# Weights on the sync queue in column blocks, a layer norm in three lagged steps, and one product for the memory read, in a fused attention and gated-MLP block

## The chip, the cores and the metric

The kernel runs on one core of one Trainium2 chip. The metric is device time in microseconds of one execution; the time before is the median of three runs. The engines in the profile are PE (matmul), PEld (its weight loads), DVE (vector), ACT (scalar activations), POOL (GpSimd) and SP (which here only issues transfers; SPq and ACTq are the queues of SP and ACT).

## The reference, cut to what matters

The input x has 2048 tokens of 1024 channels, in bfloat16. With 32 heads of width 32 and four segments of 512 tokens:

```python
h = x + A(layernorm(x));  out = h + B(layernorm(h))

# A, for each segment s: causal softmax attention inside the segment, and a linear memory over earlier ones
p = softmax(q_s k_s^T * scale + mask);  a_dot = p v_s
a_mem = (phi(q_s) M) / (phi(q_s) z + 1e-6)          # phi(t) = t+1 if t>0 else exp(t)
o = g * a_mem + (1 - g) * a_dot                      # g = sigmoid(beta), one per head
M += phi(k_s)^T v_s;  z += sum(phi(k_s))             # afterwards: A returns o @ wo

# B, with F = 3584, Fh = 1792
z = gelu(x @ w_in);  z1 = z[:, :Fh];  z2 = layernorm(z[:, Fh:])
return (z1 * (w_sp @ z2 + b_sp)) @ w_out
```

## The kernel before

Every operation is recorded by a small helper (so that all of them carry line 209 in the profile), which derives the waits from the memory cells that an operation reads and writes; a PSUM bank of 2 KB is one cell, so engines that touch different columns of a bank still wait for each other. Each engine runs its own operations in the order of recording. The order of the code is thus the order on each engine, and nothing is rearranged.

**Start.** `x_load` brings chunks of 128 tokens into `XCH` on SP; the weights are issued on ACT's queue, whole or in halves. For the four chunks of segment 0, `ln_stats` takes mean and variance on DVE and the reciprocal root on POOL, `ln_apply` normalizes on DVE, `pe_T` transposes on PE with an eviction by ACT into `XNT`, and `proj_v` makes half of V. `gates` prepares the gate masks.

**Attention loop.** The loop over n = 0..31 takes eight rounds for each of four segments (s, c = divmod(n, 8)); a round treats four heads. In a round, in this order: `logits(n, 0)`, the key product for round n+1, `pv(n-1, 2)` with the output norm of the round before (`norm`, on DVE), a pop of the background list, `logits(n, 1)`, the query product for n+1, `pv(n, 0)`, `logits(n, 2)` with the memory read (`mem` on PE, `mem_norm` on DVE, from segment 1 on), the list f3, `phi(n+1)`, `pv(n, 1)`, a pop, `state(n)` (the memory update), the list f4, a pop. Logits of four key blocks stand in banks 0 to 3, the values' products in banks 4 and 5; the projections and the state rotate over banks 6 and 7. Each `logits` is followed by an exponential on ACT (tiles e_99, e_100, e_101 for parts 0, 1, 2) and causal masks on POOL (`affine_select`). `mem` uses columns 256 on of banks 0 to 2, whose first 256 columns hold part 2 of the logits: for each of four query blocks one product with 128 columns for the numerator and one with four for the denominator.

f3 and f4 hold the V halves of this or the next segment (`proj_v`), and the output projection of the segment before (`wo`, halves of 512 columns), which adds x (`XR`), stores h, and hands the chunk to a layer norm whose transpose lands in `HNT`. In the first four rounds of segments 0 to 2, a chunk of the next segment is loaded and handed to the same background list:

```python
def ln_tasks(src, dst, tcl):
    box = {}
    bg.append(lambda: box.__setitem__("k", ln_stats(src)))
    bg.append(lambda: to_T(dst, tcl, ln_apply(src, box["k"])))
```

`bg_pop` runs one entry. `to_T` is a transposing transfer issued by SP. SP also issues the key transposes at the end of `phi`, the x loads, the stores of h, and the w_in blocks (`win_load`).

**Feed-forward part.** After the loop, `z2_group(k, tc)` multiplies a chunk of normalized h by 448 columns of w_in (eight matmuls), applies gelu on ACT, and takes statistics on DVE, for 4 x 16 groups; the last wo pieces of segment 3 stand between groups 5 to 8 of the first pass. Then come the z1 products, the product with w_sp, and w_out. Tiles of this part lie over those of the attention part in SBUF.

Of the kernel before, what the change touches and what calls it, by code (L numbers as in the profile page):

```python
# [18 lines left out]
NTC = T // 128  # L19
NQ = 8  # L20
SCALE = 32 ** (-0.5)
LN_EPS = 1e-5
MEM_EPS = 1e-6
# [234 lines left out]
def bass_sequential_preLN__memory_aug_infini_attn__mixer_gmlp__prompt_kernel(  # L258
# [43 lines left out]
    cb = Bump(0, 14 * K)  # L302
# [11 lines left out]
    STATS = [cb("stats%d" % i, [128, 2, 6], F32) for i in range(2)]  # L314
    MV = [cb("mv%d" % i, [128, 2], F32) for i in range(2)]
    RS = [cb("rs%d" % i, [128, 2], F32) for i in range(2)]
    RD = cb("rd", [128, 4, 4], F32)
    RDM = cb("rdm", [128, 4, 4], F32)

# [3 lines left out]
    XNT = [tens("xnT0", [128, 8, L], BF16, 30 * K), tens("xnT1", [128, 8, L], BF16, 38 * K)]  # L323
# [7 lines left out]
    LNO = [b1("lno%d" % i, [128, D], BF16) for i in range(3)]  # L331
    OT = b1("oT", [128, NQ, L], BF16)
    b2 = Bump(134 * K, ARENA)
    XCH = [b2("xch%d" % i, [128, D], BF16) for i in range(3)]
    QK = [b2("qk%d" % i, [128, 2, L], BF16) for i in range(3)]
    PQK = [b2("pqk%d" % i, [128, 2, L], BF16) for i in range(3)]
    ETMP = b2("etmp", [128, 2, L], BF16)
# [3 lines left out]
    TM = b2("tm", [128, 4, 4, 32], F32)  # L341
# [29 lines left out]
    def next_bank():  # L371
        b = rot["banks"][rot["n"] % len(rot["banks"])]
        rot["n"] += 1
        return b

    def mm8(dst, lhs, rhs, n=8):
        for i in range(n):
            pe.matmul(dst, lhs(i), rhs(i), start=(i == 0), stop=(i == n - 1))


    def x_load(tc):
        sp.dma_start(XCH[tc % 3][:], x2d[tc * 128:(tc + 1) * 128, :])
# [12 lines left out]
    act.dma_start(WO[:], wcols(A_wo, 0, D))  # L395


    pool.memset(MHALF[:], -0.5)
# [22 lines left out]
    lnc = [0]  # L421

    def ln_stats(src):
        k = lnc[0] % 2
# [93 lines left out]
    def mem(n):  # L518
        c = n % NQ
        for cq in range(4):  # L520
            pq = PQK[n % 3][:, 0, cq * 128:(cq + 1) * 128]
            o = 256 + (cq % 2) * 128
            pe.matmul(PS[:, cq // 2, o:o + 128], pq, MZB[:, c, :, 0:32], start=True, stop=True)
            pe.matmul(PS[:, 2, 256 + cq * 4:260 + cq * 4], pq, MZB[:, c, :, 32], start=True, stop=True)

    def mem_norm(n):
        dve.tensor_single_scalar(RDM[:], PS[:, 2, 256:272].rearrange("p (q i) -> p q i", i=4), float(MEM_EPS),
                                 ALU.add)
        dve.reciprocal(RDM[:], RDM[:])
        om = PS[:, 0:2, 256:512].rearrange("p b (h i d) -> p b h i d", h=2, i=4)  # L530
# [50 lines left out]
    bg = []  # L581

    def ln_tasks(src, dst, tcl):
        box = {}
        bg.append(lambda: box.__setitem__("k", ln_stats(src)))
        bg.append(lambda: to_T(dst, tcl, ln_apply(src, box["k"])))

    def bg_pop(k=1):
        for _ in range(k):
            if bg:  # L590
                bg.pop(0)()


    ks = {}
    ks[0] = ln_stats(XCH[0])
# [16 lines left out]
    def win_load(k):  # L612
        kind, lo, w = CH[k]
        sp.dma_start(WIN[k % 3][:, :, 0:w], wcols(B_w_in, lo, lo + w))


    LAST = NSEG * NQ - 1
    for n in range(LAST + 1):
        s, c = divmod(n, NQ)
        f3, f4 = [], []  # L620
        if s == 0:
            f3 = [("v", 0, c, 1)] if c < 4 else [("v", 1, c - 4, 0)]
        elif s < NSEG - 1:
            if c < 2:
                f3, f4 = [("v", s, 2 * c, 1)], [("v", s, 2 * c + 1, 1)]
            elif c < 6:
                f3, f4 = [("wo", s - 1, c - 2, 0)], [("wo", s - 1, c - 2, 1)]
            else:
                f3, f4 = [("v", s + 1, 2 * (c - 6), 0)], [("v", s + 1, 2 * (c - 6) + 1, 0)]
        else:  # L630
            if c < 4:
                f3 = [("v", s, c, 1)]
            wl = {2: [0], 3: [1], 4: [2], 5: [3], 6: [4, 5], 7: [6, 7]}.get(c, [])
            for u in wl:
                f4.append(("wo", s - 1, u // 2, u % 2))

        def fill(lst):
            for u in lst:
                (proj_v if u[0] == "v" else wo)(*u[1:])

        if s < NSEG - 1 and c < 4:
            x_load(4 * (s + 1) + c)
            ln_tasks(XCH[(4 * (s + 1) + c) % 3], XNT[(s + 1) % 2], c)
        if s > 0 and c == 1:
            xr_load(4 * (s - 1))

        logits(n, 0)
        if n < LAST:
            proj_qk(n + 1, 1)
        if n > 0:  # L650
            pv(n - 1, 2)
        bg_pop()
        logits(n, 1)
        if n < LAST:
            proj_qk(n + 1, 0)
# [13 lines left out]
    xr_load(4 * (NSEG - 1))  # L669


    rot["banks"] = list(range(8))
    win_load(2)

    def wsp_load(tb):
# [4 lines left out]
    zq = []  # L680

    def z2_group(k, tc):
        s, tcl = divmod(tc, 4)
        b = next_bank()
        wi = WIN[k % 3]
        mm8(PS[:, b, 0:448], lambda i: HNT[s][:, i, tcl * 128:(tcl + 1) * 128], lambda i: wi[:, i, 0:448])
        z = Z2[:, tc, k * 448:(k + 1) * 448]
        act.activation(z, PS[:, b, 0:448], ACTF.Gelu_apprx_tanh)
        dve.bn_stats(ZST[:, tc, k, :], z)
        if k == 3:  # L690
            dve.bn_aggr(ZMV[:, tc, :], ZST[:, tc, :, :])
            pool.tensor_single_scalar(ZRS[:, tc:tc + 1], ZMV[:, tc, 1:2], float(LN_EPS), ALU.add)
            pool.tensor_tensor(ZRS[:, tc:tc + 1], ZRS[:, tc:tc + 1], MHALF[:], ALU.pow)
            zq.append(tc)

    def z2_apply():
        tc = zq.pop(0)
        dve.tensor_scalar(Z2[:, tc, :], Z2[:, tc, :], ZMV[:, tc, 0:1], ZRS[:, tc:tc + 1], ALU.subtract, ALU.mult)

    for k in range(4):  # L700
        for tc in range(NTC):
            z2_group(k, tc)
            if k == 0:
                bg_pop()
                if 5 <= tc < 9:
                    wo(NSEG - 1, tc - 5, 0)
                    wo(NSEG - 1, tc - 5, 1)
                    bg_pop()
            if len(zq) > 1:
                z2_apply()  # L710
        if k + 3 < 8:
            win_load(k + 3)
        assert not bg
    for k in range(4, 8):
        lo, w = CH[k][1:]
        for fl in range(w // 128):
# [64 lines left out]
```

## Time and profile before

| | |
|---|---|
| median of 3 runs | 865.43 us (862.6 to 865.89) |
| profiled execution | 867.66 us, its span 865.9 us |
| PE busy | 802.0 us, 93% of the span |
| DVE, ACT, POOL busy | 382.9, 302.2, 121.8 us |
| start until the first logits | 38.22 us |
| attention loop, to the first w_in product | 38.22 to 363.54 us |
| feed-forward part | 363.54 to 865.90 us |

A row of the timeline has the start, the duration, the engine, the line, the operation, the tile written and those read (buffer numbers belong to the tile's number: e_99, e_100 and e_101 are three buffers), the count where neighbours are merged, and in brackets the idle time before it with what ended it. A wait is read from the brackets; whether it costs anything is read from PE, whose idle time alone makes the end later. PE's time for a merged group runs to the end of the last matmul's pipeline, so two groups behind one another take less than the sum.

### The profile page before, as it was taken

What the parts mean: (1) busy time and instruction counts of PE and PEld (TensorE: products, weight loads), DVE (VectorE), ACT (ScalarE), POOL (GpSimd) and SP (SyncE); (2) the same over time, 40 slices, a digit from 0 to 9 for tenths busy, and PEclk for the clock granted to TensorE, in tenths of its full rate; (3) what the DMA queues carried; (4) which work ended last, traced back from release to release, by engine and by line L of the source; (5) the groups of instructions that cost most, each with busy time, mean ns of one, the idle gap of its engine ahead of it and who ended that gap; (6) DMA issues with size and microseconds to landing.
All of it is one profiled execution on the core that took longest, in us unless ns stands there. A gap on an engine that the chain in (4) does not pass through costs nothing.

```text
span 865.9 us, 12541 instructions
## 1 busy us (share of the span) xinstructions
PE 802.0 (93%) x5354; PEld 390.6 (45%) x5440; DVE 382.9 (44%) x777; ACT 302.2 (35%) x351; POOL 121.8 (14%) x234
## 2 busy tenths in 40 slices
PE   1787988899889999699999999999999999999998
PEld 0343544444444555345555444444444444444443
DVE  4153347876787456665446400005314323432432
ACT  1566866677667778313333333310000000000000
POOL 2033322332233324100003200000000000000000
PEclk9998999999999999899999999999999999999999
DMA  8422042435343304373100420056035026002002
GB/s 317 138 62 50 20 93 67 111 73 86 81 109 71 75 6 134 81 168 101 49 21 29 122 48 1 1 178 108 7 90 105 0 62 139 1 31 73 1 7 79
DMA packets 122728, 64.79 MB, mean 75 GB/s; under 512 B 94768, under 2 KB 109616, under 8 KB 122672
## 3 DMA queue, kind: packets, MB, share of 16 engines
q1 hardware_dynamic: 117472, 55.60, 26.9%
q10 hardware_dynamic: 5200, 8.39, 2.7%
q8 instruction: 42, 0.69, 0.3%
q14 instruction: 14, 0.11, 0.0%
HBM read 32.51 MB, written 8.39 MB: 47 GB/s over the span
## 4 chain that ended last, share of the span: by engine, by line
PE 78%; DVE 7%; ACT 5%; POOL 3%; DMA 3%; ACTq 2%; issue 2%; SPq 1%
PE ps L209 78%; ACTq L209 2%; POOL e_100 L209 2%; DMA xch_87<-in_A_x_dram 1%; ACT e_99 L209 1%; DVE stats_59 L209 1%; ACT v L209 1%; ACT e_100 L209 1%; SPq L209 1%; DVE stats_60 L209 1%; DMA xch_88<-in_A_x_dram 1%; ACT etmp L209 1%; POOL rs_63 L209 1%; DVE etmp L209 1%; ACT e_101 L209 0%
## 5 line engine op out<-in xcount | busy, mean ns | idle before, releaser
L209 PE MATMUL ps<-w_out,yT 128*128 128x512 bf16 x439 | 96.9, 379 | 0.5
L209 PE MATMUL ps<-wspT_113,z_110 128*128 128x512 bf16 x439 | 96.5, 379 | 0.5
L209 PE MATMUL ps<-wspT_112,z_110 128*128 128x512 bf16 x439 | 96.5, 379 | 0.5
L209 ACT ACTIVATE e_99<-ps 128x2048 bf16<-128x2048 f32 x32 | 60.0, 1875 | 45.9 <-PE ps L209 45.9
L209 PEld LDWEIGHTS ps<-wspT_113,z_110 128*128 128x128 bf16 x448 | 43.9, 98 | 52.8
L209 PEld LDWEIGHTS ps<-wspT_112,z_110 128*128 128x128 bf16 x448 | 43.8, 98 | 52.9
L209 PEld LDWEIGHTS ps<-w_out,yT 128*128 128x128 bf16 x448 | 43.8, 98 | 52.9
L209 ACT ACTIVATE z_110<-ps 128x448 bf16<-128x448 f32 x64 | 34.8, 543 | 85.2 <-PE ps L209 85.2
L209 DVE TENSOR_TENSOR tmpg_119<-ps,brow_117 128x512 f32<-128x512 f32 x14 | 9.7, 690 | 116.7 <-DMA brow_117<-in_B_b_sp_dram 96.4
L209 PE MATMUL ps<-wo,oT 128*128 128x512 bf16 x241 | 57.7, 385 | 3.8 <-DVE hch_80 L209 1.2
L209 ACT ACTIVATE e_100<-ps 128x2048 bf16<-128x2048 f32 x32 | 60.1, 1877 | 0.8 <-PE ps L209 0.7
L209 DVE BATCH_NORM_STATS2 zst<-z_110 128x6 f32<-128x448 bf16 x64 | 39.8, 622 | 41.5 <-ACT z_110 L209 41.5
L209 ACT ACTIVATE z1T<-ps 128x512 bf16<-128x512 f32 x56 | 33.4, 597 | 63.3 <-PE ps L209 63.3
L209 PE MATMUL ps<-wv,xnT_71 128*128 128x512 bf16 x121 | 30.5, 396 | 16.1 <-ACT xnT_71 L209 15.2
L209 POOL TENSOR_SCALAR_AFFINE_SELECT e_100<-e_100 128x512 bf16<-128x512 bf16 x64 | 41.1, 666 | 26.6 <-ACT e_100 L209 26.6
L209 PE MATMUL ps<-v,e_100 128*128 128x33 bf16 x512 | 22.4, 178 | 17.4 <-POOL e_100 L209 16.9
L209 PEld LDWEIGHTS ps<-wo,oT 128*128 128x128 bf16 x256 | 23.7, 99 | 29.4 <-issue 1.9
L209 ACT ACTIVATE e_101<-ps 128x1024 bf16<-128x1024 f32 x32 | 32.7, 1023 | 11.0 <-PE ps L209 10.7
L209 PE MATMUL ps<-xnT_71,wk 128*128 128x512 bf16 x125 | 32.7, 409 | 1.6 <-DVE msum L209 0.9
L209 POOL TENSOR_SCALAR_AFFINE_SELECT e_99<-e_99 128x512 bf16<-128x512 bf16 x32 | 20.5, 639 | 95.7 <-ACT e_99 L209 95.7
L209 ACT ACTIVATE v<-ps 128x512 bf16<-128x512 f32 x32 | 19.1, 597 | 40.3 <-PE ps L209 40.3
L209 PE MATMUL ps<-xnT_72,wk 128*128 128x512 bf16 x126 | 30.0, 380 | 1.3 <-DVE msum L209 0.9
(187 smaller groups left out, 1103.3 us busy)
## 6 DMA issues: line engine op xcount, KB each, us to landing
w_out<-in_B_w_out_dram SPq DMA_DIRECT2D x1, 3584.0 KB, 13.0
wv<-in_A_wv_dram ACTq DMA_DIRECT2D x2, 1024.0 KB, 14.0
wk<-in_A_wk_dram ACTq DMA_DIRECT2D x1, 2048.0 KB, 14.5
wq<-in_A_wq_dram ACTq DMA_DIRECT2D x1, 2048.0 KB, 19.3
wo<-in_A_wo_dram ACTq DMA_DIRECT2D x1, 2048.0 KB, 17.3
xr_77<-in_A_x_dram SPq DMA_DIRECT2D x8, 256.0 KB, 3.0
xr_78<-in_A_x_dram SPq DMA_DIRECT2D x8, 256.0 KB, 3.1
win_107<-in_B_w_in_dram SPq DMA_DIRECT2D x2, 896.0 KB, 4.7
```

Of the source, the lines that this page charges most:

```text
L209: ins = getattr(e, op.name)(*op.args, **op.kw)
```

## The change

- Start: x chunks 0 and 1, then the first half of wv, chunks 2 and 3, the first 256 columns of wk and of wq, beta, and the rest of the weights, all issued by SP in this order. `XCH` has four buffers instead of three, so the tiles laid out behind it move by 2 KB. Statistics of chunks 0 and 1 stand ahead of the first apply.
- Layer norm in the loop: three lists, one for each step (statistics; reciprocal root on POOL; apply and transpose). Each pop runs one entry of each list, the oldest step first, so a chunk's three steps lie one pop apart. Statistics tiles have four buffers instead of two.
- Memory read: one product of 132 columns for each query block (numerator and denominator side by side), in banks 0 to 3; in `mem_norm` one multiply over four blocks instead of two over two.
- Last segment: the wo pieces of rounds 28, 29 stand in f3 instead of f4, those of round 30 in f3 and f4 instead of both in f4; in round 31 the wo pieces stand where the next round's key and query products would, and the first two w_in groups in f3 and f4.
- After the loop the banks rotate from 6, 7, 0, 1 on; the first pass begins with group 2; w_in statistics run behind by two groups; there is one more pop between the wo halves.

```diff
-    XCH = [b2("xch%d" % i, [128, D], BF16) for i in range(3)]
+    XCH = [b2("xch%d" % i, [128, D], BF16) for i in range(4)]
...
     x_load(0)
+    x_load(1)
+    sp.dma_start(WV[:, :, 0:512], wcols(A_wv, 0, 512))
+    x_load(2)
+    x_load(3)
+    sp.dma_start(WK[:, :, 0:256], wcols(A_wk, 0, 256))
+    sp.dma_start(WQ[:, :, 0:256], wcols(A_wq, 0, 256))
     sp.dma_start(BETAB[:], A_beta.partition_broadcast(128))
-    x_load(1)
-    x_load(2)
-    act.dma_start(WV[:, :, 0:512], wcols(A_wv, 0, 512))
-    act.dma_start(WK[:], wcols(A_wk, 0, D))
-    act.dma_start(WQ[:], wcols(A_wq, 0, D))
-    act.dma_start(WV[:, :, 512:1024], wcols(A_wv, 512, D))
-    act.dma_start(WO[:], wcols(A_wo, 0, D))
+    sp.dma_start(WV[:, :, 512:1024], wcols(A_wv, 512, D))
+    sp.dma_start(WK[:, :, 256:D], wcols(A_wk, 256, D))
+    sp.dma_start(WQ[:, :, 256:D], wcols(A_wq, 256, D))
+    sp.dma_start(WO[:], wcols(A_wo, 0, D))
...
         dve.bn_aggr(MV[k][:], STATS[k][:])
+        return k
+
+    def ln_rstd(k):
         pool.tensor_single_scalar(RS[k][:, 0:1], MV[k][:, 1:2], float(LN_EPS), ALU.add)
         pool.tensor_tensor(RS[k][:, 1:2], RS[k][:, 0:1], MHALF[:], ALU.pow)
-        return k
...
         for cq in range(4):
-            pq = PQK[n % 3][:, 0, cq * 128:(cq + 1) * 128]
-            o = 256 + (cq % 2) * 128
-            pe.matmul(PS[:, cq // 2, o:o + 128], pq, MZB[:, c, :, 0:32], start=True, stop=True)
-            pe.matmul(PS[:, 2, 256 + cq * 4:260 + cq * 4], pq, MZB[:, c, :, 32], start=True, stop=True)
+            pe.matmul(PS[:, cq, 256:388], PQK[n % 3][:, 0, cq * 128:(cq + 1) * 128], MZB[:, c, :, 0:33],
+                      start=True, stop=True)
...
-        for b in range(2):
-            dve.tensor_tensor(TM[:, 2 * b:2 * b + 2, :, :], om[:, b, :, :, :],
-                              RDM[:, 2 * b:2 * b + 2, :].unsqueeze(3).to_broadcast([128, 2, 4, 32]), ALU.mult)
+        dve.tensor_tensor(TM[:], om[:, :, :, 0:32], RDM[:].unsqueeze(3).to_broadcast([128, 4, 4, 32]), ALU.mult)
...
+    def bg_pop():
+        if lnq[2]:
+            src, dst, tcl, k = lnq[2].pop(0)
+            to_T(dst, tcl, ln_apply(src, k))
+        if lnq[1]:
+            it = lnq[1].pop(0)
+            ln_rstd(it[3])
+            lnq[2].append(it)
+        if lnq[0]:
+            it = lnq[0].pop(0)
+            lnq[1].append(it + (ln_stats(it[0]),))
...
+    stats_of(0)
+    stats_of(1)
     for tc in range(4):
-        o = ln_apply(XCH[tc % 3], ks[tc])
-        if tc < 3:
-            if tc == 0:
-                x_load(3)
-            ks[tc + 1] = ln_stats(XCH[(tc + 1) % 3])
+        o = ln_apply(XCH[tc], ks[tc])
+        if tc < 2:
+            stats_of(tc + 2)
...
-            wl = {2: [0], 3: [1], 4: [2], 5: [3], 6: [4, 5], 7: [6, 7]}.get(c, [])
-            for u in wl:
-                f4.append(("wo", s - 1, u // 2, u % 2))
+            if c in (2, 3):
+                f4 = [("wo", s - 1, 0, c - 2)]
+            elif c in (4, 5):
+                f3 = [("wo", s - 1, 1, c - 4)]
+            elif c == 6:
+                f3, f4 = [("wo", s - 1, 2, 0)], [("wo", s - 1, 2, 1)]
+            elif c == 7:
+                f1, f2 = [("wo", s - 1, 3, 0)], [("wo", s - 1, 3, 1)]
+                f3, f4 = [("z2", 0, 0)], [("z2", 0, 1)]
...
-    rot["banks"] = list(range(8))
+    rot["banks"] = [6, 7, 0, 1, 2, 3, 4, 5]
+    rot["n"] = 0
...
-        for tc in range(NTC):
+        for tc in range(2 if k == 0 else 0, NTC):
             z2_group(k, tc)
             if k == 0:
                 bg_pop()
                 if 5 <= tc < 9:
                     wo(NSEG - 1, tc - 5, 0)
+                    bg_pop()
                     wo(NSEG - 1, tc - 5, 1)
                     bg_pop()
+            z2_stats()
```

More of the change, by code (lines that the diff above doesn't have):

```diff
@@ L313, in bass_sequential_preLN__memory_aug_infini_attn__mixer_gmlp__prompt_kernel @@
     MHALF = cb("mhalf", [128, 1], F32)
-    STATS = [cb("stats%d" % i, [128, 2, 6], F32) for i in range(2)]
-    MV = [cb("mv%d" % i, [128, 2], F32) for i in range(2)]
-    RS = [cb("rs%d" % i, [128, 2], F32) for i in range(2)]
+    STATS = [cb("stats%d" % i, [128, 2, 6], F32) for i in range(4)]
+    MV = [cb("mv%d" % i, [128, 2], F32) for i in range(4)]
+    RS = [cb("rs%d" % i, [128, 2], F32) for i in range(4)]
     RD = cb("rd", [128, 4, 4], F32)
@@ L381, in x_load @@
     def x_load(tc):
-        sp.dma_start(XCH[tc % 3][:], x2d[tc * 128:(tc + 1) * 128, :])
+        sp.dma_start(XCH[tc % 4][:], x2d[tc * 128:(tc + 1) * 128, :])
     def wcols(ap, lo, hi):
@@ L423, in ln_stats @@
     def ln_stats(src):
-        k = lnc[0] % 2
+        k = lnc[0] % 4
         lnc[0] += 1
@@ L579, in wo, with stats_of @@
             ln_tasks(HCH[tc % 3], HNT[s], tcl)
-    bg = []
+    lnq = [[], [], []]
     def ln_tasks(src, dst, tcl):
[L584 to L591, printed above, removed]
-    ks = {}
-    ks[0] = ln_stats(XCH[0])
-    for tc in range(4):
-        o = ln_apply(XCH[tc % 3], ks[tc])
-        if tc < 3:
-            if tc == 0:
-                x_load(3)
-            ks[tc + 1] = ln_stats(XCH[(tc + 1) % 3])
+        lnq[0].append((src, dst, tcl))
+    def bg_pop():
[9 more added lines that the diff above has]
+            lnq[1].append(it + (ln_stats(it[0]),))
+    ks = {}
+    def stats_of(tc):
+        ks[tc] = ln_stats(XCH[tc])
+        ln_rstd(ks[tc])
+    stats_of(0)
+    stats_of(1)
+    for tc in range(4):
+        o = ln_apply(XCH[tc], ks[tc])
+        if tc < 2:
+            stats_of(tc + 2)
         pe_T(XNT[0], tc, o)
@@ L614, in win_load, with z2_group, z2_stats, z2_apply @@
         sp.dma_start(WIN[k % 3][:, :, 0:w], wcols(B_w_in, lo, lo + w))
+    zs, zq = [], []
+    def z2_group(k, tc):
+        s, tcl = divmod(tc, 4)
+        b = next_bank()
+        wi = WIN[k % 3]
+        mm8(PS[:, b, 0:448], lambda i: HNT[s][:, i, tcl * 128:(tcl + 1) * 128], lambda i: wi[:, i, 0:448])
+        act.activation(Z2[:, tc, k * 448:(k + 1) * 448], PS[:, b, 0:448], ACTF.Gelu_apprx_tanh)
+        zs.append((k, tc))
+    def z2_stats():
+        k, tc = zs.pop(0)
+        dve.bn_stats(ZST[:, tc, k, :], Z2[:, tc, k * 448:(k + 1) * 448])
+        if k == 3:
+            dve.bn_aggr(ZMV[:, tc, :], ZST[:, tc, :, :])
+            pool.tensor_single_scalar(ZRS[:, tc:tc + 1], ZMV[:, tc, 1:2], float(LN_EPS), ALU.add)
+            pool.tensor_tensor(ZRS[:, tc:tc + 1], ZRS[:, tc:tc + 1], MHALF[:], ALU.pow)
+            zq.append(tc)
+    def z2_apply():
+        tc = zq.pop(0)
+        dve.tensor_scalar(Z2[:, tc, :], Z2[:, tc, :], ZMV[:, tc, 0:1], ZRS[:, tc:tc + 1], ALU.subtract, ALU.mult)
     LAST = NSEG * NQ - 1
@@ L619, in bass_sequential_preLN__memory_aug_infini_attn__mixer_gmlp__prompt_kernel @@
         s, c = divmod(n, NQ)
-        f3, f4 = [], []
+        f1, f2, f3, f4 = [], [], [], []
+        if n < LAST:
+            f1, f2 = [("qk", n + 1, 1)], [("qk", n + 1, 0)]
         if s == 0:
@@ L632, in bass_sequential_preLN__memory_aug_infini_attn__mixer_gmlp__prompt_kernel @@
                 f3 = [("v", s, c, 1)]
-            wl = {2: [0], 3: [1], 4: [2], 5: [3], 6: [4, 5], 7: [6, 7]}.get(c, [])
-            for u in wl:
-                f4.append(("wo", s - 1, u // 2, u % 2))
+            if c in (2, 3):
[7 more added lines that the diff above has]
+                f3, f4 = [("z2", 0, 0)], [("z2", 0, 1)]
         def fill(lst):
             for u in lst:
-                (proj_v if u[0] == "v" else wo)(*u[1:])
+                {"v": proj_v, "wo": wo, "qk": proj_qk, "z2": z2_group}[u[0]](*u[1:])
         if s < NSEG - 1 and c < 4:
             x_load(4 * (s + 1) + c)
-            ln_tasks(XCH[(4 * (s + 1) + c) % 3], XNT[(s + 1) % 2], c)
+            ln_tasks(XCH[c], XNT[(s + 1) % 2], c)
         if s > 0 and c == 1:
@@ L647, in bass_sequential_preLN__memory_aug_infini_attn__mixer_gmlp__prompt_kernel @@
         logits(n, 0)
-        if n < LAST:
-            proj_qk(n + 1, 1)
+        fill(f1)
         if n > 0:
@@ L653, in bass_sequential_preLN__memory_aug_infini_attn__mixer_gmlp__prompt_kernel @@
         logits(n, 1)
-        if n < LAST:
-            proj_qk(n + 1, 0)
+        fill(f2)
         pv(n, 0)
@@ L678, in wsp_load @@
             sp.dma_start_transpose(WSPT[tb % 2][:, :, tcl * 128:(tcl + 1) * 128], B_w_sp[r:r + 128, :])
[L680 to L698, printed above, removed]
     for k in range(4):
-        for tc in range(NTC):
+        for tc in range(2 if k == 0 else 0, NTC):
             z2_group(k, tc)
@@ L712, in bass_sequential_preLN__memory_aug_infini_attn__mixer_gmlp__prompt_kernel @@
             win_load(k + 3)
-        assert not bg
+        assert k == 0 or not any(lnq)
+    while zs:
+        z2_stats()
     for k in range(4, 8):
```

5 lines of the change are left out of this document (2 added, 3 removed).

## The prediction

> **What bounds the kernel now.** I read the page first (busy shares, the chain of waits), then a table by stage, then one by round of the attention loop, then the timeline of the start, of one round and of the turn into the feed-forward part.
>
> ```profile
> span 865.9 us, 12541 instructions
> PE 802.0 (93%) x5354; PEld 390.6 (45%) x5440; DVE 382.9 (44%) x777; ACT 302.2 (35%) x351; POOL 121.8 (14%) x234
> PE 78%; DVE 7%; ACT 5%; POOL 3%; DMA 3%; ACTq 2%; issue 2%; SPq 1%
> ```
>
> PE is the bound by share, but a fifth of the chain runs over other things. The stage table says where (columns: stretch, its length, then busy time and count of PE, PEld, DVE, ACT, POOL, then granted clock, DMA share, GB/s). The rows are: start; segments 0, 1, 2 of eight rounds each; the last segment without and then with only its last round; the rest.
>
> ```profile
> 0.00:38.22 38.22, 14.93 (x79) 7.20 (x81) 11.84 (x31) 8.80 (x13) 4.38 (x18) 1.00 0.70 247
> 38.22:112.43 74.21, 64.35 (x653) 33.42 (x666) 30.28 (x80) 55.20 (x57) 23.87 (x40) 0.93 0.21 44
> 112.43:201.73 89.30, 79.64 (x790) 41.47 (x801) 64.09 (x145) 58.84 (x57) 27.01 (x48) 0.98 0.37 83
> 201.73:287.68 85.95, 78.42 (x790) 40.98 (x802) 63.65 (x147) 58.03 (x56) 27.03 (x48) 1.00 0.42 87
> 348.90:363.54 14.64, 7.98 (x89) 4.09 (x89) 9.72 (x22) 6.06 (x4) 4.04 (x8) 0.88 0.23 55
> 363.54:865.90 502.36, 497.29 (x2330) 232.10 (x2368) 167.75 (x266) 68.18 (x120) 16.13 (x40) 1.00 0.25 62
> ```
>
> The last 502 us are dense PE work that the change only shortens by two groups. Everything else happens in the first 363.5 us. By round:
>
> ```profile
> 48.03:57.81 9.78, 7.70 (x86) 4.17 (x87) 5.56 (x13) 6.93 (x7) 3.49 (x7) 0.99 0.33 70
> 97.13:104.78 7.65, 7.49 (x86) 4.03 (x86) 2.69 (x8) 6.82 (x9) 2.49 (x4) 1.00 0.09 19
> 112.43:126.49 14.06, 11.06 (x101) 5.69 (x102) 9.14 (x20) 8.24 (x9) 3.56 (x6) 0.88 0.56 113
> 137.08:149.44 12.36, 9.91 (x100) 5.19 (x102) 8.52 (x20) 7.24 (x7) 3.37 (x6) 1.00 0.31 76
> 149.44:159.90 10.46, 9.77 (x100) 5.05 (x101) 9.11 (x21) 6.76 (x6) 3.42 (x6) 1.00 0.62 140
> 191.68:201.73 10.05, 9.82 (x100) 5.06 (x101) 5.04 (x14) 7.85 (x8) 2.49 (x4) 1.00 0.07 15
> 338.79:348.90 10.11, 9.59 (x97) 4.94 (x98) 8.30 (x20) 6.34 (x6) 3.60 (x6) 1.00 0.64 170
> ```
>
> These are rounds 1, 6, 8, 10, 11, 15 and 30. Round 6 does the same PE work as round 1 (86 matmul records) without a layer norm: 7.65 against 9.78. So a layer-norm round pays about 2 us, round 8 about 4.
>
> **The start.** ACT issues the weights and can compute nothing until it is through; x chunk 1 arrives late because the weights share the engines.
>
> ```profile
> 4.11 1.42 DVE L209 BATCH_NORM_STATS2 stats_59<-xch_86 128x6 f32<-128x512 bf16 x2 [2.57 <-DMA xch_86<-in_A_x_dram]
> ...
> 7.39 1.04 PE L209 MATMUL ps<-ident,lno_82 128*128 128x128 bf16 x8 [7.39 <-DVE lno_82 L209]
> 9.96 1.42 DVE L209 BATCH_NORM_STATS2 stats_60<-xch_87 128x6 f32<-128x512 bf16 x2 [2.62 <-DMA xch_87<-in_A_x_dram]
> ...
> 12.26 5.31 ACTq L209 DMA_DIRECT2D wo<-in_A_wo_dram  x1
> ...
> 17.60 1.28 ACT L209 ACT_TABLE_LOAD   x1 [17.60 <-issue]
> ...
> 18.89 1.02 ACT L209 ACTIVATE xnT_71<-ps 128x1024 bf16<-128x1024 bf16 x1
> ...
> 19.97 3.60 PE L209 MATMUL ps<-wv,xnT_71 128*128 128x512 bf16 x8 [11.54 <-ACT xnT_71 L209]
> ```
>
> With the weights on SP, ACT is free at once and loads its table under the first x. Statistics of chunks 0 and 1 now both stand before the first apply on DVE: 4.1 + 2 x (1.42 + about 0.2) = 7.4, apply 0.55 (row below) to 7.95, eight transposes 1.04 to 9.0, eviction 1.02 to 10.1, first V product 10.15 instead of 19.97: **-9.8 us**. Behind it the order is as now. Data must hold up: x0, x1 and the first WV block are 1.6 MB.
>
> ```profile
> 2.00:4.00 2.00, 0.00 (x0) 0.00 (x0) 0.00 (x0) 0.00 (x0) 0.00 (x0) 1.00 0.89 219
> 4.00:6.00 2.00, 0.00 (x0) 0.00 (x0) 1.60 (x3) 0.00 (x0) 0.13 (x1) 1.00 0.85 297
> ```
>
> At 219 to 297 GB/s from 2.0 us on, x1 is there by 4.4 and WV by 7.6 to 9; slack 1 to 2.5 us. SP now carries some 17 us of issuing (the last of ACT's ends at 12.26 + 5.31); behind it stand the first key transpose and chunk 4's load, not due before 29. All nine MB, at 247 GB/s over the first 38.2 us, have landed by then too, so I price that at nothing; were it late by d, rounds 0 and 1 would be. Bounds: -5.6 (x1 as late as 9.96, then 1.6 + 0.55 + 1.04 + 1.02 more) to -10.5.
>
> The row of x1 against later loads is the point: issued among the weights it landed 8 us after its issue, in the rounds (below) 3. [...]
>
> **Layer norm in three steps.** One round of the timeline:
>
> ```profile
> 43.67 1.42 DVE L209 BATCH_NORM_STATS2 stats_59<-xch_87 128x6 f32<-128x512 bf16 x2 [4.21 <-DMA xch_87<-in_A_x_dram]
> ...
> 45.73 0.57 POOL L209 TENSOR_TENSOR rs_63<-rs_63,mhalf 128x1 f32<-128x1 f32 x1
> ...
> 46.26 1.27 POOL L209 TENSOR_SCALAR_AFFINE_SELECT e_100<-e_100 128x512 bf16<-128x512 bf16 x2
> ...
> 46.95 0.27 PE L209 MATMUL ps<-v,e_100 128*128 128x33 bf16 x4 [1.48 <-POOL e_100 L209]
> ...
> 47.73 0.85 DVE L209 TENSOR_SCALAR lno_83<-xch_87,mv_61,rs_63 128x1024 bf16<-128x1024 bf16 x1
> ...
> 49.07 1.31 SPq L209 DMA_TRANSPOSE xnT_72<-lno_83  x1
> ...
> 50.42 0.58 SPq L209 DMA_DIRECT2D xch_88<-in_A_x_dram  x1
> ...
> 53.39 1.42 DVE L209 BATCH_NORM_STATS2 stats_60<-xch_88 128x6 f32<-128x512 bf16 x2 [1.59 <-DMA xch_88<-in_A_x_dram]
> ```
>
> And from the waits, longest first (total, times, longest):
>
> ```profile
> PE ps L209 <- POOL e_100 L209: 16.9, 21, 3.3
> ```
>
> Now DVE waits for x, POOL's reciprocal root waits for DVE, the mask of e_100 stands behind it on POOL, and PE waits for the mask: 16.9 us in all (last row), plus the slow clock after a long one (clock 0.88 in round 8). The change puts the root one pop later, behind both e_100 masks: that wait goes. Late next is DVE itself: statistics still stand in the same place, waiting for the same load, and behind them the memory norm, the wo additions, phi and the state copies. The apply goes behind the state copies, and SP's next x load is behind its transpose. The loop from statistics to statistics, 9.72 us now (43.67 to 53.39), is then statistics 1.6, phi about 1.0 and state copies 0.6 (estimates: round 6 holds these and the norm in 2.69 of DVE), apply 0.55 to 0.85, transpose issue 1.31, load to statistics 2.97: 8.1 to 8.4, against a clean round of 7.65. It lags 0.5 us more each round and reaches PE (through the two rotating banks) in rounds 2 to 4: I take 7.85, 7.7, 8.0, 8.35, 8.3 and three of 7.65 = 63.2 for 74.2: **-11.0** (bounds -6, each x round 1.2 more, to -13, none late).
>
> Segments 1 and 2: the x statistics end about 7.7 us into a round, 0.7 to 1 after the last exponential, so the memory norm is late, then the wo addition, for which the second wo waits (one bank). In rounds with both kinds of layer norm DVE also gets 10.8 us (9.11 in round 11 plus an apply and a statistics). I take 10.2, 10.3, 11.5, 11.3, 10.8, 10.15, 9.7, 9.8 = 83.7 for 89.3: **-5.6**. Round 11 gets worse, 8, 10 and 12 better. Segment 2 starts undisturbed and gives 83.2 for 85.95: **-2.7**. Bounds together: 0 to -13.
>
> **Memory as one product.** Half the matmuls and weight loads in front of the last exponential, one multiply instead of two behind it:
>
> ```profile
> 335.96 0.48 PE L209 MATMUL ps<-mzb,pqk_94 128*128 128x128 bf16 x8
> ...
> 336.48 1.02 ACT L209 ACTIVATE e_101<-ps 128x1024 bf16<-128x1024 f32 x1 [0.43 <-PE ps L209]
> ...
> 338.03 0.75 DVE L209 TENSOR_TENSOR tm<-ps,rdm 128x256 f32<-128x256 f32 x2
> ```
>
> Four of eight save about 0.2, the multiply under 0.1 (only the two starts merge): 0.25 a round, inside the figures above, and in the last segment, where this chain sets the round, 6 x 0.25 = 1.5. Round 30 has both wo pieces after the last product; one moved ahead covers the chain: 0.4. **-1.9** (bounds 0 to -3).
>
> **Last round.**
>
> ```profile
> 363.54 7.91 PE L209 MATMUL ps<-win_107,hnT_67 128*128 128x448 bf16 x32 [3.22 <-DVE ta L209]
> ...
> 364.23 5.37 SPq L209 DMA_TRANSPOSE oT<-otok_106  x4
> ...
> 371.28 3.19 PE L209 MATMUL ps<-win_107,hnT_68 128*128 128x448 bf16 x16
> ```
>
> Now PE is busy 7.98 of 14.64 us and starts w_in late, as its bank is one that the norm still reads. Then: eight products of 448 columns are 1.55 (3.19 for sixteen, less the tail), so of 512 about 1.75; round 30's 9.59 less four of these leaves 2.6 for logits and values; two wo 3.5, two w_in 3.1: 9.2, and 9.75 with the small gaps; it goes straight on in banks 6 and 7. Gain: 14.64 - 9.75 = 4.9, two groups of 1.55 less behind, and no slow clock (7.91 against 2 x 3.19: 1.5): 9.5. The first wo of segment 3 comes four groups (6.2 us) after the loop instead of six, against some 2.5 until DVE has the norm (it has an apply and a statistics, 2.2, ahead of it) and about 4 for a transpose (four take 5.37 to issue; 2.97 for a load's way): 0.4 of waiting. **-9.1** (bounds -5 to -11). Lagged w_in statistics, the moved tiles and the fourth x buffer cost nothing under 502 us of PE with DVE at 168; without that cover a late statistics would hold the next bank's release.
>
> [...]
>
> **Sum.** 9.8 + 11.0 + 5.6 + 2.7 + 1.9 + 9.1 = 40.1. The profiled execution took 867.66 (span 865.9), 2.2 above the median 865.43: 827.6 there, 825 as a median.
>
> **Rivals.**
> A. The wait moves instead of going: x statistics block DVE so long that the memory norm and phi hold PE as POOL did. For it: the loop is hardly shorter than a round, DVE has 9.1 of 10.46 in wo rounds. Against: the bank of the state copies is next needed some 2.7 us into the following round. Segments 0 to 2 then give 7 instead of 19.3: 837.
> B. x1 still shares with the weights: start -5.6, 829.
> C. No wait reaches PE: -13, -7.5, -4.7 in the segments: 819.
> D. Slower: the lagged apply, transpose and load on SP make the x loop longer than now. At 9.72 the 19.3 of the segments is gone and 20.8 (start, last segment, last round) is left; past 9.72 each of the twelve x rounds adds its excess, so it decides at 9.72 + 20.8 / 12 = 11.45, and a loop of 11.8 gives 865.4 - 20.8 + 12 x 2.1 = 870. For it: on SP the transpose now waits for the state copies and stands behind the key transpose. Against: the parts add up to 8.4 at most.
> E. The change does not do what it says: the root moves but e_100 was late for its own exponential. Round 6 has no such wait; as A.
>
> **Numbers.** Likeliest (819 to 832) 0.60 with B inside, A 0.22, C and better 0.13, D 0.03, unchanged 0.02. Range: C with the best start and tail, 813, to A with the poor start, 842. 0.5% (4.3 us) is about what a measurement of this kernel tells from no change. Faster 0.95, same 0.02, slower 0.03.
>
> **What would show it.** First V product near 10 us and round 0 near 28.5; no PE wait for e_100 in x rounds; segments near 63, 84, 83; PE dense in the last round, w_in going on within 1 us. Wrong if x1 starts late, if DVE waits for x reach PE's logits, or if PE stands before the first wo of segment 3.

## The result, and the profile after

The changed kernel takes 827.0 us (median of 4 runs, 826.17 to 828.59) against 864.96 us before: ratio 0.9567, 95% interval 0.9543 to 0.9592. The profiled execution has a span of 825.4 us, 40.5 less than before.

From the page of the changed kernel: the span, PE's row and that of the others, and the chain that ended last.

```profile
span 825.4 us, 12334 instructions
PE 787.2 (95%) x5258; PEld 384.3 (47%) x5344; DVE 368.6 (45%) x753; ACT 301.8 (37%) x351; POOL 120.8 (15%) x234
PE 80%; DVE 9%; DMA 5%; ACT 3%; issue 2%; SPq 1%; POOL 0%
```

PE's busy time fell by 15 us: slow matmuls and half of the memory products are gone. The rest of the 40.5 us was waiting. POOL, 3% of the chain before, is out of it; DVE and the x loads have more of it. The same stages as before (columns: stretch, length, busy time and count of PE, PEld, DVE, ACT, POOL, granted clock, DMA share, GB/s):

```profile
0.00:28.79 28.79, 15.21 (x79) 7.46 (x82) 11.40 (x31) 8.91 (x13) 4.92 (x18) 1.00 0.94 305
28.79:91.02 62.23, 59.75 (x654) 31.68 (x667) 28.46 (x80) 54.58 (x57) 24.10 (x40) 1.00 0.27 63
91.02:174.75 83.73, 76.52 (x759) 39.75 (x771) 58.97 (x137) 58.94 (x57) 26.12 (x48) 1.00 0.40 89
174.75:258.85 84.10, 76.52 (x757) 39.77 (x769) 59.01 (x139) 58.10 (x56) 26.17 (x48) 1.00 0.40 89
258.85:318.67 59.82, 57.62 (x604) 30.60 (x615) 35.19 (x83) 47.03 (x47) 19.28 (x32) 1.00 0.34 83
318.67:329.50 10.83, 10.83 (x111) 6.00 (x111) 9.08 (x20) 7.24 (x7) 4.04 (x8) 1.00 0.28 82
```

| stage | before | after | predicted change | measured change |
|---|---|---|---|---|
| start, to the first logits | 38.22 | 28.79 | -9.8 | -9.4 |
| segment 0 | 74.21 | 62.23 | -11.0 | -12.0 |
| segment 1 | 89.30 | 83.73 | -5.6 | -5.6 |
| segment 2 | 85.95 | 84.10 | -2.7 | -1.9 |
| last segment without its last round | 61.22 | 59.82 | -1.9 | -1.4 |
| last round and all behind it | 517.00 | 506.73 | -9.1 | -10.3 |
| sum | 865.90 | 825.40 | -40.1 | -40.5 |

The last row of the view ends at 329.50, 1.8 us into the w_in groups that follow the loop; the last round itself ends at 327.70, 9.03 us after its start. The clock column tells a part of the gain: 0.93, 0.98 and 0.88 in three stages before, 1.00 everywhere now.

**The start**, from the timeline (start, duration, instruction, idle time before it and what ended that):

```profile
0.79 1.28 ACT L209 ACT_TABLE_LOAD   x1 [0.79 <-PEq L789]
...
3.32 1.42 DVE L209 BATCH_NORM_STATS2 stats_59<-xch_92 128x6 f32<-128x512 bf16 x2 [1.77 <-DMA xch_92<-in_A_x_dram]
...
4.90 1.37 DVE L209 BATCH_NORM_STATS2 stats_60<-xch_93 128x6 f32<-128x512 bf16 x2
...
6.98 1.03 PE L209 MATMUL ps<-ident,lno_88 128*128 128x128 bf16 x8 [6.98 <-DVE lno_88 L209]
...
8.05 1.02 ACT L209 ACTIVATE xnT_77<-ps 128x1024 bf16<-128x1024 bf16 x1 [5.98 <-PE ps L209]
8.09 3.25 SPq L209 DMA_DIRECT2D betab<-in_A_beta_dram  x1
10.27 3.57 PE L209 MATMUL ps<-wv,xnT_77 128*128 128x512 bf16 x8 [2.26 <-DMA wv<-in_A_wv_dram]
```

ACT's table is loaded at once. The statistics of chunk 1 follow those of chunk 0 without a gap, where chunk 1 came at 9.96 before. The first V product starts at 10.27, and what it waits for last is its weight.

**A layer-norm round**, round 0, from the same view:

```profile
33.56 1.22 POOL L209 TENSOR_SCALAR_AFFINE_SELECT e_107<-e_107 128x512 bf16<-128x512 bf16 x2 [1.74 <-ACT e_107 L209]
...
35.05 1.42 DVE L209 BATCH_NORM_STATS2 stats_59<-xch_92 128x6 f32<-128x512 bf16 x2 [5.01 <-DMA xch_92<-in_A_x_dram]
...
35.68 0.56 PE L209 MATMUL ps<-v,e_107 128*128 128x33 bf16 x16
...
36.80 0.22 POOL L209 TENSOR_SCALAR rs_67<-mv_63 128x1 f32<-128x1 f32 x1 [1.02 <-DVE mv_63 L209]
```

The masks (e_107 here, e_100 before) wait for their exponential alone and are done before DVE has begun the statistics; PE takes all sixteen value products in one go, with no idle bracket. The statistics wait longer for x than before, 5.01 us against 4.21, and in segment 0 this costs about 1 us (the run with x loaded a round earlier, below).

**What is left**, in a wo round of segment 2, and in the list of PE's waits from the first logits to the last round (total, times, longest):

```profile
201.06 1.42 DVE L209 BATCH_NORM_STATS2 stats_61<-xch_94 128x6 f32<-128x512 bf16 x2 [1.19 <-DMA xch_94<-in_A_x_dram]
...
203.08 0.69 DVE L209 TENSOR_TENSOR tm<-ps,rdm 128x512 f32<-128x512 f32 x1
...
203.69 0.68 DVE L209 TENSOR_TENSOR hch_86<-xr_83,ps 128x512 bf16<-128x512 bf16 x1
...
204.65 1.67 PE L209 MATMUL ps<-wo,oT 128*128 128x512 bf16 x7 [1.26 <-DVE hch_86 L209]
```

```profile
PE ps L209 <- DVE hch_86 L209: 3.0, 3, 1.3
PE ps L209 <- DVE msum L209: 2.9, 5, 0.8
PE ps L209 <- DVE hch_87 L209: 2.7, 2, 1.9
PE ps L209 <- DVE hch_85 L209: 2.5, 3, 1.1
```

DVE goes through statistics, memory norm and addition in one run, and the second wo waits for the addition: a load that is late on DVE reaches PE through a PSUM bank (1.26 us here). Before, the waits for POOL were 16.9 us; now 8.2 us are waits for wo additions.

**The last round:**

```profile
324.06 1.68 PE L209 MATMUL ps<-win_114,hnT_73 128*128 128x448 bf16 x8
...
325.98 1.67 PE L209 MATMUL ps<-win_114,hnT_73 128*128 128x448 bf16 x8
...
327.70 3.19 PE L209 MATMUL ps<-win_114,hnT_73 128*128 128x448 bf16 x16
...
333.96 3.40 PE L209 MATMUL ps<-wo,oT 128*128 128x512 bf16 x15
```

Two w_in groups lie in the round, the next two follow it with no gap and in 3.19 us, as in the kernel before at a clock of 1.00, and the first wo piece of segment 3 starts where PE comes to it.

### The profile page after: what moved, and what is told of

Same layout as the page of the kernel before. It is cut to its first block, busy times and chain, and to the rows that moved or that the text cites. A ratio compares the mean times of both kernels' runs of the same rounds, so it can differ in the third digit from the quotient of the medians.

```text
span 825.4 us, 12334 instructions
## 1 busy us (share of the span) xinstructions
PE 787.2 (95%) x5258; PEld 384.3 (47%) x5344; DVE 368.6 (45%) x753; ACT 301.8 (37%) x351; POOL 120.8 (15%) x234
## 4 chain that ended last, share of the span: by engine, by line
PE 80%; DVE 9%; DMA 5%; ACT 3%; issue 2%; SPq 1%; POOL 0%
PE ps L209 80%; DMA xch_93<-in_A_x_dram 1%; DMA xch_95<-in_A_x_dram 1%; DMA xch_94<-in_A_x_dram 1%; DMA wv<-in_A_wv_dram 1%; ACT e_108 L209 1%; DVE stats_60 L209 1%; DVE stats_62 L209 1%; DVE rdm L209 1%; SPq L209 1%; ACT v L209 1%; DVE tm L209 1%; ACT etmp L209 1%; DVE etmp L209 1%; DVE stats_59 L209 1%
## 5 line engine op out<-in xcount | busy, mean ns | idle before, releaser
L209 POOL TENSOR_SCALAR_AFFINE_SELECT e_107<-e_107 128x512 bf16<-128x512 bf16 x64 | 39.6, 643 | 46.9 <-ACT e_107 L209 46.9
L209 POOL TENSOR_SCALAR_AFFINE_SELECT e_106<-e_106 128x512 bf16<-128x512 bf16 x32 | 20.3, 634 | 126.9 <-ACT e_106 L209 126.9
L209 ACT ACTIVATE e_108<-ps 128x1024 bf16<-128x1024 f32 x32 | 32.7, 1023 | 10.5 <-PE ps L209 10.3
L209 PE MATMUL ps<-xnT_78,wk 128*128 128x512 bf16 x125 | 29.7, 380 | 2.1 <-DVE msum L209 1.6
L209 PE MATMUL ps<-xnT_77,wk 128*128 128x512 bf16 x125 | 29.7, 380 | 2.0 <-DVE msum L209 1.3
L209 PE MATMUL ps<-xnT_77,wq 128*128 128x512 bf16 x120 | 28.8, 380 | 1.2 <-issue 0.8
## 6 DMA issues: line engine op xcount, KB each, us to landing
w_out<-in_B_w_out_dram SPq DMA_DIRECT2D x1, 3584.0 KB, 13.4
```

Of the source, the lines that this page charges most:

```text
L209: ins = getattr(e, op.name)(*op.args, **op.kw)
```

## The experiments

The theory: four separate waits went (ACT held by issuing; PE held by POOL's masks; PE idle in the last round; the memory chain), and what is left in the layer-norm rounds is DVE held by x. The main rival: the waits only moved, or another part of the change did it. Medians are compared with the 827.0 of the changed kernel; each run also had the kernel before beside it, and ratios are to that. The kernel before gave medians from 864.9 to 866.9 us there, so a difference of 2 us between medians says little by itself, and the rounds in the traces carry the argument where differences are small.

**The start undone.** All x loads and beta on SP, the weights on ACT as before:

```diff
...
-    sp.dma_start(WV[:, :, 0:512], wcols(A_wv, 0, 512))
...
+    act.dma_start(WV[:, :, 0:512], wcols(A_wv, 0, 512))
+    act.dma_start(WK[:], wcols(A_wk, 0, D))
+    act.dma_start(WQ[:], wcols(A_wq, 0, D))
+    act.dma_start(WV[:, :, 512:1024], wcols(A_wv, 512, D))
+    act.dma_start(WO[:], wcols(A_wo, 0, D))
```

> The changed kernel with the weights issued by ACT again, whole and in the old order (x loads and beta stay on SP). My theory: only the start goes back, by the 9.4 us that separate the first logits (38.2 before, 28.8 after): 836.4, ACT's first work at 17.6 us, the first V product near 20, attention segments unchanged (62, 84, 84). Rival (the start is bound by the late x1, not by ACT's issuing): ACT is still done issuing at 17.6, but nothing waits for that, and the first V product comes near 14: 831. Rival (a busy weight ring slows the first rounds too): segment 0 also changes by over 1 us.

Measured: 836.54 us, 9.5 more (ratio to the kernel before 0.9668, 0.9636 to 0.97). From its timeline:

```profile
17.43 1.28 ACT L209 ACT_TABLE_LOAD   x1 [17.43 <-issue]
18.73 1.02 ACT L209 ACTIVATE xnT<-ps 128x1024 bf16<-128x1024 bf16 x1
...
19.80 3.59 PE L209 MATMUL ps<-wv,xnT 128*128 128x512 bf16 x8 [7.38 <-ACT xnT L209]
```

PE had the transposes done at 12.4 (11.39 + 1.04) and waited 7.38 us for ACT, which was still issuing. So ACT's issuing bound the start, and the late x1 (its statistics began at 9.25) only stood inside it. Segment 0 is 61.92 us: its rounds are not touched.

**The root early.** The reciprocal root in the pop of the statistics, everything else as changed:

```diff
-            ln_rstd(it[3])
             lnq[2].append(it)
...
             lnq[1].append(it + (ln_stats(it[0]),))
+            ln_rstd(lnq[1][-1][3])
```

> The changed kernel with the reciprocal root on POOL issued in the same pop as the statistics again, ahead of the e_100 masks; apply stays two pops behind. My theory (the gain of the attention segments is the wait of PE for POOL's masks): the waits of PE for the e_100 masks come back, some 12 to 17 us in total, segment 0 goes to 71 to 75, segments 1 and 2 to 86 to 90: 845 to 855. Rival (the gain came from the lag of the apply or the fourth x buffer): unchanged, 827 within 2.

Measured: 849.43 us, 22.4 more (ratio 0.9826, 0.9777 to 0.9875). PE's waits, and segments 0 and 1:

```profile
PE ps L209 <- POOL e L209: 22.3, 24, 2.4
```

```profile
28.00:101.95 73.95, 64.80 (x664) 33.08 (x665) 29.88 (x81) 55.17 (x57) 23.73 (x40) 0.95 0.27 59
101.95:193.87 91.92, 82.17 (x770) 41.04 (x769) 64.22 (x137) 58.87 (x57) 26.76 (x48) 0.96 0.37 81
```

The wait for the masks is back, at 22.3 us larger than before, and so is the slow clock. Segment 1 (91.92) and segment 2 (88.22) are slower than in the kernel before (89.30 and 85.95): with the root early, the lag of the apply and the fourth x buffer gain nothing, and the memory read's share is lost too. The waits came to more than the 12 to 17 us that I expected, and segment 1 to more than its 90.

**Only the root late.** The kernel before, with the two POOL instructions moved one pop on and nothing else:

```diff
-    bg.append(lambda: to_T(dst, tcl, ln_apply(src, box["k"])))
+    bg.append(lambda: (ln_rstd(box["k"]), to_T(dst, tcl, ln_apply(src, box["k"]))))
...
```

> The kernel before with one edit: the reciprocal root is issued in the next pop, just ahead of the apply, instead of with the statistics. Start, memory read, last round and the three x buffers stay old. My theory: most of the gain of segments 0 to 2 (19.4 us in the full change, of which some 4 belong to the memory read) is in this edit alone: segments near 63, 86, 85.5: 849 to 853. Rival (the lag of the apply is needed, since DVE then waits for POOL): under 6 us of gain, 859 or more.

Measured: 851.51 us (ratio 0.9845, 0.9817 to 0.9873). PE's wait for the masks, and segments 0 to 2:

```profile
PE ps L209 <- POOL e L209: 0.3, 1, 0.3
```

```profile
38.36:101.30 62.94, 59.23 (x652) 31.90 (x665) 29.06 (x80) 54.70 (x57) 24.19 (x40) 1.00 0.24 52
101.30:188.95 87.65, 78.78 (x790) 40.77 (x801) 60.32 (x145) 58.96 (x57) 26.44 (x48) 0.98 0.39 85
188.95:273.07 84.12, 77.19 (x789) 40.45 (x801) 59.97 (x147) 58.14 (x56) 26.48 (x48) 1.00 0.42 89
```

The wait for the masks falls from 16.9 to 0.3 us. The segments take together 14.8 us less than before, of the 19.4 of the full change; all of segment 0's gain but 0.7 is in these two instructions. POOL's own work is the same; only its place in the queue differs.

**The old memory read:**

```diff
-            pe.matmul(PS[:, cq, 256:388], PQK[n % 3][:, 0, cq * 128:(cq + 1) * 128], MZB[:, c, :, 0:33],
+            pe.matmul(PS[:, cq // 2, o:o + 128], pq, MZB[:, c, :, 0:32], start=True, stop=True)
+            pe.matmul(PS[:, 2, 256 + cq * 4:260 + cq * 4], pq, MZB[:, c, :, 32], start=True, stop=True)
...
```

> The changed kernel with the old memory read (eight products in three banks, two multiplies). My theory: 0.25 us a round in 24 rounds, less where PE is not held by that chain: the last segment's rounds 27 to 29 go from 7.9 to 8.15, total 3 to 6 us: 831. Rival (PE has spare time in those rounds, only the last segment shows it): 1.5 us, 828.5.

Measured: 833.17 us, 6.2 more (ratio 0.9634, 0.9602 to 0.9667), just above the range. The last segment without its last round gives back 0.8 us, segments 1 and 2 2.7 and 2.5: 86.41 and 86.64. Rounds that x does not disturb pay 0.14 us (rounds 12 and 13: 10.47 against 10.33), less than the 0.25 of the theory. The slowest round of each segment, with both kinds of layer norm, has 13.42 and 12.99 against 11.27 and 11.70. But such rounds also differ between runs that have the same code there: round 19 took 10.99 in the run with the start undone and 13.29 in the next one. So the total is measured, and its split over the rounds, and why these rounds should pay more, is not shown.

**The last segment as before**, with the new order of banks kept:

```diff
+            wl = {2: [0], 3: [1], 4: [2], 5: [3], 6: [4, 5], 7: [6, 7]}.get(c, [])
...
-        for tc in range(2 if k == 0 else 0, NTC):
+        for tc in range(NTC):
...
```

> The changed kernel with the last segment's wo pieces and the w_in groups placed as before (all sixteen w_in groups of the first pass after the loop). My theory: the last round and what follows go back by some 9 us, of which 1 to 2 are a slow clock after PE's idling, and round 30 by 0.5: 836 to 837. Rival (the wait for the output transposes ahead of the first wo is what counts, and the bank order already removed half of the idle time): 831 to 832.

Measured: 832.84 us, 5.8 more (ratio 0.9628, 0.9596 to 0.966): between the two. The first w_in products after the loop:

```profile
331.48 9.24 PE L209 MATMUL ps<-win,hnT 128*128 128x448 bf16 x48
```

They start 10.67 us after the last round's beginning (320.81), against 14.64 before. They follow the last value products (which end at 331.5) at once, where the kernel before idled 3.22 us for the norm: with the banks taken from 6 and 7 on they need none that the norm reads. So this wait goes without any work moved into the round; what the moved work removes is the idling inside the round (here PE is busy 8.1 of the 11.2 us from 320.8 to 332, at a clock of 0.85), and about 0.4 us in round 30 (9.71 here, 9.36 in the changed kernel).

**Only the first block of wv on ACT's queue:**

```diff
-    sp.dma_start(WV[:, :, 0:512], wcols(A_wv, 0, 512))
+    act.dma_start(WV[:, :, 0:512], wcols(A_wv, 0, 512))
```

> The changed kernel with only the first half of wv on ACT's queue, all else on SP. The first V product waited 2.3 us for it, although by then 2.6 MB had moved and it is within the first 1.6 MB in ring order. Theory 1 (on one ring it shares the engines with what is issued behind it): on its own ring it lands about 1.5 to 2 us earlier, x1 a little later, and the start gains 1: 826. Theory 2 (the ring takes its transfers in order, and the block is slow by its short rows): it lands at the same time, 827, or x1 later by 2 and the start 1 to 2 longer, 828.5.

Measured: 829.29 us (ratio 0.9592, 0.9567 to 0.9615), as in the last alternative of theory 2. From its timeline and its transfers:

```profile
6.98 1.42 DVE L209 BATCH_NORM_STATS2 stats<-xch 128x6 f32<-128x512 bf16 x2 [1.29 <-DMA xch<-in_A_x_dram]
...
11.26 3.60 PE L209 MATMUL ps<-wv,xnT 128*128 128x512 bf16 x8 [1.12 <-ACT xnT L209]
```

```profile
wv<-in_A_wv_dram ACTq DMA_DIRECT2D x1, 1024.0 KB, 7.8
```

Chunk 1's statistics start at 6.98 instead of 4.90 (4.90 to 5.37 in the eight kernels here that have the changed start), and the V product at 11.26 (9.32 to 10.32 there). So with the block on a queue of its own chunk 1 came 1.6 to 2.1 us later. How much of the 2.3 us this is stays open, since this profile also has a slow second V product (3.57 us for 1.90; see the last section). The block itself landed 7.8 us after an issue at 0.78, so at 8.6. With all on SP the first V product waits for it in four of the eight profiles, by 1.46 to 2.26 us, and starts at 9.89 to 10.32; in the other four it starts at 9.32 to 9.60 without that wait. That a queue of its own brings the block earlier is thus not shown, and what its short rows do was not tried.

**x loaded a round earlier:**

```diff
+    x_load(4)
     for n in range(LAST + 1):
...
-            x_load(4 * (s + 1) + c)
             ln_tasks(XCH[c], XNT[(s + 1) % 2], c)
+        s1, c1 = divmod(n + 1, NQ)
+        if s1 < NSEG - 1 and c1 < 4:
+            x_load(4 * (s1 + 1) + c1)
```

> The changed kernel with each x chunk loaded one round earlier, so that no statistics wait for a load. My theory (what is left of the layer-norm rounds' cost is DVE held by x statistics, behind which the memory norm and the wo addition stand): segment 0 to 61.2, rounds 10, 11, 18, 19 from 11 to 11.7 down to 10.3 to 10.6, 5 us in all: 822. Rival (DVE's own work is the bound in these rounds, not the load): under 1.5 us, 826.

Measured: 821.88 us, 5.1 less (ratio to the kernel before 0.9509, 0.9486 to 0.9531). Segments 0 to 2:

```profile
30.22:91.40 61.18, 59.22 (x652) 31.89 (x666) 28.43 (x80) 54.58 (x57) 23.44 (x40) 1.00 0.27 61
91.40:173.33 81.93, 76.51 (x758) 39.72 (x769) 59.55 (x137) 58.89 (x57) 26.23 (x48) 1.00 0.41 91
173.33:254.96 81.63, 76.52 (x758) 39.76 (x771) 59.37 (x139) 58.07 (x56) 26.21 (x48) 1.00 0.40 88
```

DVE's work is unchanged and segment 0 runs at 7.65 us a round throughout; rounds 10, 11, 18 and 19 take 10.33 to 10.48, as expected. The load, not DVE's amount of work, was what the layer norms still cost.

**The memory norm behind the wo addition**, in the wo rounds:

```diff
...
-        logits(n, 2)
+        late = NQ <= n < 3 * NQ and 2 <= c < 6
+        logits(n, 2, late)
         fill(f3)
+        if late:
+            mem_norm(n)
```

> The changed kernel with the memory norm recorded behind f3 in the wo rounds of segments 1 and 2, so that the first wo addition stands ahead of it on DVE. My theory (the second wo waits for the bank that the first addition frees): the waits of PE for the additions, 8.2 us in the loop, mostly go; 4 to 6 us: 822. Rival (the next logits then wait for the late memory norm instead): 826 to 829.

Measured: 829.78 us, 2.8 more (ratio 0.9596, 0.9577 to 0.9616). My theory fell, and the rival's wait was another one:

```profile
PE ps L209 <- DVE msum L209: 9.9, 13, 1.2
```

The waits for the additions fell to 1.7 us, those for the state copies (msum) rose from 2.9 to 9.9. phi stands behind the memory norm and the state copies behind phi, and the next round's key product takes the bank that they free. Rounds that x does not disturb show it: rounds 12 and 14 take 10.88 and 10.77, against 10.33 and 9.81.

**The second pop behind the state update**, with x early:

```diff
         pv(n, 1)
-        bg_pop()
         state(n)
+        bg_pop()
```

> The kernel with early x loads (previous experiment), and the second pop of a round recorded behind the state update, so that an apply stands behind the state copies on DVE and not ahead of them. My theory: rounds 15 and 23 (10.42 us, PE waiting 0.56 for the state copies) go to 9.9, little else moves: 820 to 821. Rival (those rounds are held by the exponential chain): unchanged, 822.

Measured: 820.42 us (ratio 0.9471, 0.9447 to 0.9496). Rounds 15 and 23 go from 10.42 to 9.96 and 9.97, as expected, and PE's waits for the state copies, 1.1 us in the run with early loads alone, are gone from its list. The two rounds are 0.9 us; the medians differ by 1.5.

**The wo rounds reordered**, with x early:

```diff
...
+        if both:
+            pv(n, 1)
+            fill(f4)
         if n < LAST:
             phi(n + 1)
...
+        if not both:
+            pv(n, 1)
...
+        bg_pop(s == NSEG - 1)
...
```

Here `both` marks the wo rounds of segments 1 and 2, and the argument says whether statistics may start in this pop.

> Early x loads, and the wo rounds of segments 1 and 2 reordered: values part 1, then the second wo, then phi, state and a pop for apply and root only; statistics only in the first pop of a round (segments 0 to 2). The second wo takes the bank of the query product, free early, and the state takes the bank that the first wo addition frees. My theory (the second wo waits 0.5 to 0.8 us a round for the first addition, and the late memory norm only handed the wait to the state copies because phi came behind both): waits for additions and for state copies both go, wo rounds from 10.33 to 9.8, rounds 15 and 23 to 9.9: 816 to 818. Rival (phi behind both additions makes key transposes and the next state late): rounds stay at 10.3 or more, 821 to 824.

Measured: 816.61 us (815.83 to 819.09), ratio 0.9432, 0.9406 to 0.9458: the fastest of all. Segments 1 and 2, and PE's wait for the additions:

```profile
88.78:168.34 79.56, 77.74 (x772) 40.10 (x771) 59.91 (x136) 58.98 (x57) 26.32 (x48) 1.00 0.46 90
168.34:247.58 79.24, 77.73 (x770) 40.08 (x770) 60.16 (x139) 58.16 (x56) 26.33 (x48) 1.00 0.47 91
```

```profile
PE ps L209 <- DVE hch L209: 1.8, 8, 0.2
```

Wo rounds take 9.73 to 9.86 us, and rounds 15 and 23 9.97 and 9.96. The waits for the state copies are gone from PE's list as well. PE is busy for 77.7 of 79.6 us: there it has become the bound.

## Why the prediction was right, and where it was not

The forecast, 825 for 827.0, rests on each stage's own wait, and the table above holds stage by stage to 1.2 us. By its steps:

- *Start.* Right in cause; that the sum fits so well is partly luck. Two steps were off and cancelled: chunk 0 came at 3.32 instead of 4.1, and wv, priced with 1 to 2.5 us to spare, was late by 2.26. Chunk 0 came at 3.32 to 3.79 in the eight kernels with the changed start, and at 4.02 where only wv has the second queue, so its gain goes with the weight that no longer runs beside it. The lower bound of 5.6, and rival B with it, needed a late chunk 1, which only appears with a second queue: its statistics began at 4.90 with all on SP, at 6.98 with the first block of wv on ACT's queue, and at 9.25 and 9.96 with all the weights there. That one queue brings chunk 1 ahead of wv was the author's assumption behind the 9.8; no run shows by what rule queues share the engines, only these four times. The first logits came between 27.6 and 30.2 us in kernels with the same start: that scatter is larger than the error made here.
- *Layer norm.* Right: the wait for POOL went and DVE's wait for x took its place. In segment 0 the sum was right for a lag that was not smaller than forecast: DVE's loop from statistics to statistics took 8.79, 8.11 and 7.98 us against the 8.1 to 8.4 of the forecast, 1.9 us of lag in all where 1.5 was taken. It cost PE a little less: rounds 0 to 4 took 7.62, 7.65, 7.91, 8.12 and 7.98 against 7.85, 7.7, 8.0, 8.35 and 8.3, which is the 12.0 for 11.0. In segments 1 and 2 the mechanism was the one described, with round 11 worse (10.46 before, 10.94 now; 11.3 was forecast) and rounds 8 and 10 better (14.06 to 10.26, 12.36 to 11.27). Segment 2's term was too large by 0.8: rounds 18 and 19 took 11.59 and 11.70, longer than before (11.00 and 10.46).
- *Memory read.* The 1.9 of the last segment was 1.4, and undoing the memory read there gives back 0.8 where 1.5 was its share. In segments 1 and 2 it stood at 0.25 a round inside the other terms, 4.0 for 16 rounds; undoing it cost 5.2 there, but undisturbed rounds only 0.14 each. The size of the step is near; its price by round is not what was forecast.
- *Last round.* Right to 1.2 us: the round took 9.03 for 9.75, and the 0.4 us of waiting before the first wo did not come. The sum did not separate the order of the banks from the moved work. The experiment gives the moved work 5.8; the 3.2 us that PE waited for the norm go without it, by the order of the banks. The slow clock of this stage was not only the matter of the 3.22 us gap: before, it fell to 0.50 at about 355 us, ahead of that gap (last section). The 1.5 us taken for it was an estimate from two rows of the kernel before, and no run shows after what idle time the clock falls; in the changed kernel sixteen w_in products took 3.19 us behind the round, at a granted clock of 1.00.
- *Rivals.* A (the wait moves and holds PE) is real but small: 5.1 us, as the early loads show. C asked that no wait reach PE, and its terms are nearly those of the kernel with early loads, although 5.4 us of waits for additions are left there: -13.0, -7.4 and -4.3 in the segments for -13, -7.5 and -4.7. D, a longer x loop, did not show: the loop was 8.0 to 8.8 us in segment 0, against 9.72 before. E (e_100 late for its own exponential) fell: with the root moved, PE's wait for the masks was 0.3 us.

## What to carry to other kernels

An instruction of under a microsecond that waits for a slow producer should not stand in a queue ahead of work that another engine waits for: moving two short POOL instructions one step on gave 13.4 us by itself, more than any other edit here. After such a move look for the next queue in which the same late thing stands, here DVE behind x, and try first to fetch the late thing earlier: that gave 5.1 us, while moving the memory norm alone lost 2.8. A reordering that also took out the next wait, for the bank freed by the state copies, gave 3.8 on top of the early loads and the later pop; without the early loads it was not tried. ACT did no work while it issued the weights (it began at 17.43 us, against 0.79 with the weights on SP), so bulk issues belong to an engine that has no work.

## What the runs showed of the hardware

The issue of beta, 8 KB spread over 128 partitions, held SP for 3.25 us, and from 12 to 14 us the engines moved only 78 GB/s (the profile's windows of the start):

```profile
12.00:14.00 2.00, 2.00 (x9) 0.88 (x8) 1.93 (x5) 0.12 (x1) 0.97 (x2) 1.00 0.66 78
```

It cost nothing here: the only transfer for which PE had a wait above 0.3 us was the first block of wv, issued ahead of it. It is the place in the queue and not the transfer that goes with the time: in the kernel before, where beta is the second issue on SP, it took 0.41 us, and behind the x chunks and the first weights 3.12 to 3.58 us in six profiles. What held the queue was not tried. The low rate that follows looks like an emptied queue (an estimate): by 12 us the engines had moved 3.08 MB, nearly all that had been issued until then (3080 KB, or 3.15 MB), and the next issue began only at 11.39 us.

The start's scatter goes largely with the second V product: in the nine profiles with the changed start (one of them with the first block of wv on ACT's queue), it took 1.90 us in five, with the first logits at 27.6 to 28.9 us, and 3.47 to 3.60 us in four, with 29.5 to 31.6. Why it runs at half pace in some executions is not shown.

How long PE stands still did not by itself tell whether its clock fell. With the root early, a wait of 2.31 us in round 0 was followed by eight key products in 1.90 us, and one of 2.37 us in round 3 by the same eight in 3.59 us (mean granted clock of the segment 0.95). In the last round of the kernel before, the clock fell to 0.50 from 355 to 358 us behind gaps of at most 1.68 us; in the run with the last segment as before it was 0.85 on average over that round's 11.2 us, behind gaps of at most 1.69 us.
